# Attention and MoE kernel: decoding of a weight tile spread over a pair, phi's transposes one pair later, last transposes between h pieces

## The chip, the core and the metric

One core of a Trainium2 chip. The kernel is one program for its engines: TensorE (PE) for matmuls and transposes, VectorE (DVE), ScalarE (ACT), GpSimd (POOL), and SyncE (SP) as the queue of most DMAs. Each engine takes its own instructions in a fixed order. The metric is the time of one execution on the device in microseconds (us), the median of several runs.

## The reference, cut to what matters

Attention with a causal softmax and a linear-attention memory, then two MLPs, all in float32. `H` = 8 heads and `B` = 4 make 32 (b, head) blocks of 576 rows; `w_in` is 512x2048, `w_out` 2048x512.

```
scores = scale * q @ k.T;  causal mask;  a = softmax(scores)
local = a @ v
phi(x) = where(x > 0, x, exp(x) - 1) + 1
mem_out = (phi(q) @ M_prev) / (phi(q) . z_prev + 1e-6)
x = g * mem_out + (1 - g) * local            # g = sigmoid(beta), 2304 rows of 512
h = x @ w_in;  y = (h * tanh(softplus(h))) @ w_out
out = ((y @ w1) * (y @ w2)) @ w3 @ w_out2
```

## The kernel before

**Stages.** The 32 blocks are 16 pairs (two heads of one b, one on each half of the partitions). A software pipeline runs over `p` = 0 to 16: while the scores of pair p are made, pair p-1 is transposed and multiplied with v. Then follow 24 units of the first MLP (4 quarters of `w_in` and `w_out` by 6 chunks of 384 tokens; `emit_h` makes h and its activation, `emit_x2` the second matmul), beside which w3 and w_out2 are multiplied (`fold`), and at the end the second MLP. A float32 matmul is three in a reduced format, so most operands exist as a high and a low part.

**A pair.** `s_blocks` (L380) and `s_last` (L396) make scores in PSUM, tile `psA`: row blocks 3, 2, then 0 and 1, then the last 64 rows of both heads (128x576, in two halves of 288). For each block DVE scales, masks and takes the row extremum (`maxed`, L372, 128x512, 384, 128, 256, 288), and ACT takes the exp and its row sum (`expd`, L377, L378). `normed` (L357) then scales each block by the gate over its sum: a short sum (L363) and reciprocal (L364) on DVE, four blocks on DVE and four on POOL (L368), and the last block (128x576) on DVE at the very end. One pair later `pt_g` (L421) transposes these blocks on PE into a bank `psF` and ACT copies them out (L430). `pv` (L432) accumulates memory and local part in `psX` and `psF`; ACT copies the high part (L451) and DVE subtracts for the low part (`xt`, L79 called from L452). `prep` (L306) transposes q and k of the next pair into `psX` (copied by ACT, L308) and makes `qd` on POOL (L314).

**Phi.** `prep_phi` (L322) works on the next pair's q: exp on ACT (L330), `phit` on POOL (L331), `phie` on DVE (L332), `qz` on POOL (L334), its row reduction `dn` on DVE (L338), `dn` + 1e-6 on POOL (L339), reciprocal and a product of 128x10 on DVE (L340, L341), and the scaled phi on POOL (L344). `trans_phi` (L349) transposes it on PE into two `psX` tiles, each copied by ACT (L351). All of it belongs to the end of p, for pair p+1.

**Decoding.** The weights come as 64-bit words and are turned into float32 by `decode` (L103): a DMA of 512 KB into `draw`, six DVE operations of 128x512 (L113, L115, L117, L120, L124, L126), one POOL addition (L131), and, for the first MLP, the rounding and subtraction on POOL that give the two parts (`to_split`, L148). The eight tiles of quarter 0 (`lq0`) are decoded at p = 3, 6, 9 and 12 in the code, one each, with one buffer, and the last four at p = 16 with a decoder of their own.

**What sets the order.** The code is written in one order, and a scheduler, from its own estimate of durations, sets the order in which each engine takes its instructions. `tc.issue_after(ins)` keeps what is issued inside it behind `ins` in that order; `in_turn` uses it to put PE's work of the pairs behind PE's last instruction. DMAs stand in SP's queue in that order too. The scheduler places the four tiles of p = 3 to 12 beside pairs 1 to 4. A `psA`, `psX` or `psF` tile is one of two buffers and is free again when the last reader of the old content is through.

## Time and profile before

| | |
|---|---|
| runs | 1026.53, 1024.01, 1025.31 us; median 1025.31 |
| profiled execution | 1024.95 us, span 1023.2, mean granted clock 0.988 |
| busy, of the span | PE 977.8 us (96%), DVE 612.0 (60%), ACT 500.7 (49%), POOL 339.0 (33%) |
| attention, first matmul of h | at 246.93 us |
| first matmul of `emit_x2` | at 277.37 us |
| chain that ended last | PE 71%, DVE 12%, ACT 11% |

Times in the trace are microseconds from the span's start. A row of the timeline has the start, the duration, engine, line, operation, output <- inputs, shape and count (a merged row holds several like it), and in brackets the idle time of that engine just before, with what ended it. A row of a window has the busy time of each engine in it, and the granted clock of PE as a share of the full one. The share of busy time over the whole span is an average over stages with different limits; the stages are read apart below.

### The profile page before, as it was taken

The page shows a single profiled execution, that of the slowest core. Times are in us where ns is not written, and L with a number is a line of the kernel's source. Part 1 is how long each engine was busy: PE and PEld are TensorE (multiplying, and loading weights), DVE is VectorE, ACT ScalarE, POOL GpSimd, SP SyncE. Part 2 cuts the span into 40 slices and gives each one's busy share as a digit, 9 for nine tenths or more (in the row PEclk, how much of TensorE's full clock was granted, in tenths as well). Part 3 has the DMA queues.
Part 4 walks back from the last instruction along what each step waited for, and adds up shares of the span by engine and source line. Part 5 has one row for each costly group of instructions (what it writes and reads, how often), then busy time and mean ns, then how long its engine had stood idle before and what let it go on. Part 6 is the DMA issues. An engine that isn't in the chain of part 4 may idle for free.

```text
span 1023.2 us, 15086 instructions
## 1 busy us (share of the span) xinstructions
PE 977.8 (96%) x5584; PEld 829.1 (81%) x5584; DVE 612.0 (60%) x1364; ACT 500.7 (49%) x1016; POOL 339.0 (33%) x345
## 2 busy tenths in 40 slices
PE   5888999999899999999999999999979999999998
PEld 2555555566799999999999999988758888888897
DVE  4887667667685759885987567667973121121111
ACT  5577888885655555556565544442313221221212
POOL 6675555433555254544454112112540000000000
PEclk9899999999999999999999999999999999999999
DMA  7343333311232124223331662222410000100101
GB/s 157 96 110 71 71 87 74 77 27 42 103 124 80 65 83 145 98 89 106 121 103 63 247 232 80 75 78 101 156 41 1 21 21 1 42 1 1 42 1 62
DMA packets 93626, 81.73 MB, mean 80 GB/s; under 512 B 68720, under 2 KB 72816, under 8 KB 93552
## 3 DMA queue, kind: packets, MB, share of 16 engines
q1 hardware_dynamic: 92224, 80.44, 25.3%
q8 instruction: 44, 0.72, 0.3%
q10 hardware_dynamic: 1328, 0.33, 0.2%
q14 instruction: 30, 0.25, 0.1%
HBM read 65.54 MB, written 15.20 MB: 79 GB/s over the span
## 4 chain that ended last, share of the span: by engine, by line
PE 71%; DVE 12%; ACT 11%; DMA 2%; POOL 2%; issue 2%; SPq 0%; POOLq 0%; ACTq 0%; DVEq 0%
PE psA L63 37%; PE psX L63 16%; PE psF L63 14%; ACT s L378 5%; ACT pt L430 3%; DVE s L368 2%; PE psF L66 2%; DMA draw<-in_moe_w_dram 1%; DVE da L120 1%; PE psX L66 1%; DVE xt L79 1%; POOL da L131 1%; DVE draw L126 1%; DVE da L117 1%; DVE s L373 1%
## 5 line engine op out<-in xcount | busy, mean ns | idle before, releaser
L63 PE MATMUL psA<-xt,wqt 128*128 128x384 f32 x1152 | 207.5, 335 | 0.2
L131 POOL TENSOR_TENSOR da<-da,draw 128x512 f32<-128x512 f32 x72 | 102.2, 1426 | 312.8 <-DVE draw L126 261.9
L63 PEld LDWEIGHTS psA<-xt,wqt 128*128 128x128 f32 x1152 | 200.0, 188 | 2.4 <-DVE y L487 0.8
L63 PE MATMUL psX<-gh,wqt 128*128 128x384 f32 x480 | 122.4, 335 | 1.1 <-DVE x L604 1.1
L749 DVE TENSOR_TENSOR bs<-bs,psA 128x512 f32<-128x512 f32 (+1 forms) x40 | 25.3, 633 | 160.0 <-ACT bs L748 160.0
L63 PE MATMUL psA<-x2h,w12t 128*128 128x512 f32 (+1 forms) x384 | 107.1, 356 | 6.9 <-DVE bs L749 4.6
L748 ACT COPY bs<-psA 128x512 f32<-128x512 f32 (+1 forms) x40 | 21.8, 545 | 162.1 <-PE psA L63 152.2
L378 ACT ACTIVATE s<-s,acc 128x512 f32<-128x512 f32 (+2 forms) x144 | 85.5, 603 | 12.8 <-DVE acc L373 12.7
L63 PE MATMUL psA<-x2s,w12t 128*128 128x512 f32 x384 | 89.6, 389 | 0.0
L63 PEld LDWEIGHTS psX<-gh,wqt 128*128 128x128 f32 x480 | 86.9, 188 | 2.3 <-DVE x L604 1.4
L477 ACT ACTIVATE y<-psA 128x384 f32<-128x384 f32 x96 | 42.0, 490 | 91.1 <-PE psA L63 91.0
L63 PEld LDWEIGHTS psA<-x2h,w12t 128*128 128x128 f32 x384 | 68.3, 189 | 20.7 <-DVE bs L749 5.0
L63 PEld LDWEIGHTS psA<-x2s,w12t 128*128 128x128 f32 x384 | 72.1, 188 | 14.9
L373 DVE CUSTOM_DVE_ANT_0 s<-psA,mask 128x512 f32<-128x512 f32 (+2 forms) x144 | 63.4, 483 | 34.4 <-PE psA L63 34.3
L63 PE MATMUL psX<-gl,wqt 128*128 128x384 f32 x240 | 80.3, 335 | 0.0
L66 PEld LDWEIGHTS psF<-ident,s 128*128 128x128 f32 x400 | 46.3, 147 | 40.8 <-ACT pt L430 24.8
L63 PE MATMUL psF<-gh,wqt 128*128 128x384 f32 x288 | 73.1, 334 | 0.0
L66 PE MATMUL psF<-ident,s 128*128 128x128 f32 x400 | 63.2, 292 | 9.9 <-ACT pt L430 7.5
L487 DVE TENSOR_TENSOR y<-y,psA 128x384 f32<-128x384 f32 x96 | 48.7, 549 | 34.9 <-ACT y L485 34.9
L63 PE MATMUL psA<-room,w12t 128*128 128x512 f32 (+1 forms) x192 | 68.0, 354 | 0.0
L368 POOL TENSOR_SCALAR s<-s,sum,ogp 128x128 f32<-128x128 f32 (+1 forms) x64 | 53.1, 840 | 37.2 <-DVE sum L364 37.2
L430 ACT COPY pt<-psF 128x512 f32<-128x512 f32 (+1 forms) x112 | 56.8, 546 | 16.0 <-PE psF L66 16.0
(114 smaller groups left out, 1878.3 us busy)
## 6 DMA issues: line engine op xcount, KB each, us to landing
draw<-in_moe_w_dram SPq DMA_DIRECT2D x32, 512.0 KB, 3.8
draw<-in_moe_w_out_dram SPq DMA_DIRECT2D x24, 512.0 KB, 3.5
draw<-in_moe_w_in_dram SPq DMA_DIRECT2D x16, 512.0 KB, 4.0
out_dram<-ob SPq DMA_DIRECT2D x18, 256.0 KB, 2.0
raw<-in_q_dram SPq DMA_DIRECT2D x32, 128.0 KB, 2.8
raw<-in_v_dram SPq DMA_DIRECT2D x32, 128.0 KB, 2.6
o_dram<-draw SPq DMA_DIRECT2D x8, 512.0 KB, 2.8
w_dram<-draw SPq DMA_DIRECT2D x8, 512.0 KB, 2.8
```

Of the source, the lines that this page charges most:

```text
L63: tail[0] = nc.tensor.matmul(o, lhsT=l, rhs=r, start=start, stop=stop).ins
L66: tail[0] = nc.tensor.transpose(o, src, ident).ins
L79: return (eng or nc.vector).tensor_tensor(out=dst, in0=src, in1=f(hi), op=ALU.subtract)
L131: nc.gpsimd.tensor_tensor(out=a, in0=a, in1=lw.bitcast(F32), op=ALU.add)
L368: (nc.gpsimd if x in ON_POOL else nc.vector).tensor_scalar(out=s, in0=s, scalar1=d["sum"][:, x:x + 1], scalar2=og[:, x:x + 1], op0=ALU.mul ...
L373: nc.vector.tensor_tensor_reduce(out=s, in0=o, in1=m, op0=ALU.add, op1=ALU.min, scale=-scale, scalar=init, accum_out=a,)
L378: nc.scalar.activation(out=s, in_=s, func=AF.Exp, scale=-1.0, bias=a, accum_out=r)
L430: nc.scalar.copy(out=t[:, 0:n], in_=o[:, 0:n])
L477: nc.scalar.activation(out=y[m // 2][:, m % 2], in_=hp[m], func=AF.Tanh, scale=0.5)
L487: nc.vector.tensor_tensor(out=y[i][:, j], in0=y[i][:, j], in1=hp[2 * i + j], op=ALU.mult)
L748: nc.scalar.copy(out=bs, in_=pb)
L749: nc.vector.tensor_tensor(out=bs, in0=bs, in1=pa, op=ALU.mult)
```

## The change

Four things are changed, all in the attention pipeline and its tail.

1. *Decoding.* `decode` is split into `fetch` (the DMA) and `decode_ops` (a list of the six DVE operations and the POOL addition). All eight tiles of quarter 0 are fetched one at a time at p = 3 to 10 and decoded at p = 4 to 11: `drip` issues one operation behind the reduces of each score block (behind `taken`, the last reduce issued), and the remaining ones at the end of the pair. The decoder has two raw buffers; no tile is decoded at p = 16.
2. *Phi.* `prep_phi(p + 1)` is placed behind the last reduce of p, `dn`'s reduction behind the last split of `pv` (`split_x`). `trans_phi(p)` runs one pair later, at the end of pair p itself, with one `psX` and one `psF` bank.
3. *The long norm* (128x576) is placed behind `split_x`.
4. *The tail.* `emit_h` is a generator `h_steps`; at p = 16 its four pieces (one of 12 matmuls for each `m`) alternate with the transposes of pair 15, and ACT's first Sin stands behind the last copy of these (`copied`).

```diff
-        for lw, hw, a, ai, _ in ts:
-            V.tensor_scalar(out=ai, in0=hw, scalar1=0x7FFFFFFF, scalar2=None, op0=ALU.bitwise_and)
...
+    def fetch(src):
+        r = dec["pool"].tile([128, dec["w"], 2], I32, tag="draw", name="draw", bufs=dec["raw"])
+        dm(out=r.rearrange("p n t -> p (n t)"), in_=src)
+        return r
...
-    decoder(at, 1, 1)
+    decoder(at, 2, 1)
...
-    def trans(src, evac):
-        for c0, c1 in ((0, 256), (256, S)):
-            pt = psX()
+    def trans(src, evac, tags="XX"):
+        for tag, (c0, c1) in zip(tags, ((0, 256), (256, S))):
+            pt = bank(tag)
...
-        nc.vector.tensor_reduce(out=dn, in_=qz, axis=mybir.AxisListType.X, op=ALU.add)
+        with ExitStack() as k_:
+            if split_x[0] is not None:
+                k_.enter_context(tc.issue_after(split_x[0]))
+            nc.vector.tensor_reduce(out=dn, in_=qz, axis=mybir.AxisListType.X, op=ALU.add)
...
-        trans(st[p]["e"], lambda cs, o: nc.scalar.copy(out=t[:, cs], in_=o))
+        trans(st[p]["e"], lambda cs, o: nc.scalar.copy(out=t[:, cs], in_=o), "XF")
...
-            if m == 1:
-                steps(beside, 1)
+            yield
...
+        with ExitStack() as k_:
+            if u == (0, 0):
+                k_.enter_context(tc.issue_after(copied[0]))
+            first = nc.scalar.activation(out=d, in_=y[1][:, 1, 0:1], func=AF.Sin, scale=0.0)
...
+    def drip(n):
+
+        if not parts and ahead:
+            r, done = ahead.pop(0)
+            ops, a, flat = decode_ops(r)
+
+            def last():
+                ops[6]()
+                done(a, flat)
+
+            parts.extend(ops[0:6] + [last])
+        with tc.issue_after(taken[0]):
+            for op in parts[:n]:
+                op()
+        del parts[:n]
...
+        decodes = 4 <= p < 12
+        if 3 <= p < 11:
+            fetch_next()
         if now:
             in_turn(s_blocks, p, (3,))
+            if decodes:
+                drip(1)
         else:
-            split = split_y((0, 0), emit_h((0, 0)))
+            in_turn(next, h0)
...
-        if not now:
-            run(lq0, 2)
-            run(lq0, 2)
+            if not now:
+                in_turn(next, h0)
...
+        if p == 1:
+            in_turn(trans_phi, 0)
...
         if p == 0:
-            in_turn(trans_phi, 0)
-        if p in (3, 6, 9, 12):
-            run(lq0, 1)
+            with tc.issue_after(taken[0]):
+                prep_phi(0)
...
+        if now:
+            with ExitStack() as k_:
+                if old:
+                    k_.enter_context(tc.issue_after(split_x[0]))
+                normed(p, [(4, None)])
+            if decodes:
+                drip(7)
         if new:
-            prep_phi(p + 1)
-            in_turn(trans_phi, p + 1)
-        if now:
-            normed(p, [(4, None)])
-    lk.close()
+            with tc.issue_after(taken[0]):
+                prep_phi(p + 1)
+        if now and p > 0:
+            in_turn(trans_phi, p)
```

How the instructions stand then, at the places that matter below. In these rows `s_998` and the like are single tiles of scores; lines are those of each kernel.

DVE at the end of a steady pair before, from the last two reduces to the next pair's first:

```order
L363 TENSOR_SCALAR sum<-sum 128x8
L364 RECIPROCAL sum<-sum 128x8
L368 TENSOR_SCALAR s_998<-s_998,sum,ogp 128x256
L368 TENSOR_SCALAR s_946<-s_946,sum,ogp 128x384
L368 TENSOR_SCALAR s_995<-s_995,sum,ogp 128x128
L368 TENSOR_SCALAR s_949<-s_949,sum,ogp 128x384
L363 TENSOR_SCALAR sum<-sum 128x1
L364 RECIPROCAL sum<-sum 128x1
L79 TENSOR_TENSOR xt_81<-psX,xt_81 128x512
L368 TENSOR_SCALAR s_113<-s_113,sum,ogp 128x576
L79 TENSOR_TENSOR xt_81<-psF,xt_81 128x64
L332 SCALAR_TENSOR_TENSOR phie<-phie,phit 128x640
```

The same place after, in a pair without decoding:

```order
L342 SCALAR_TENSOR_TENSOR phie<-phie,phit 128x640
L376 TENSOR_SCALAR sum<-sum 128x8
L377 RECIPROCAL sum<-sum 128x8
L381 TENSOR_SCALAR s_597<-s_597,sum,ogp 128x256
L381 TENSOR_SCALAR s_545<-s_545,sum,ogp 128x384
L381 TENSOR_SCALAR s_594<-s_594,sum,ogp 128x128
L381 TENSOR_SCALAR s_548<-s_548,sum,ogp 128x384
L79 TENSOR_TENSOR xt_81<-psX,xt_81 128x512
L79 TENSOR_TENSOR xt_81<-psF,xt_81 128x64
L376 TENSOR_SCALAR sum<-sum 128x1
L351 TENSOR_REDUCE dn<-qz 128x10
L377 RECIPROCAL sum<-sum 128x1
```

And after in a pair that decodes a tile (L117, L120 and L121 are decode operations):

```order
L117 SCALAR_TENSOR_TENSOR da<-draw,da 128x512
L342 SCALAR_TENSOR_TENSOR phie<-phie,phit 128x640
L376 TENSOR_SCALAR sum<-sum 128x8
L120 TENSOR_SCALAR draw<-da 128x512
L377 RECIPROCAL sum<-sum 128x8
L121 SCALAR_TENSOR_TENSOR draw<-draw 128x512
L381 TENSOR_SCALAR s_1184<-s_1184,sum,ogp 128x256
L381 TENSOR_SCALAR s_1131<-s_1131,sum,ogp 128x384
L381 TENSOR_SCALAR s_1181<-s_1181,sum,ogp 128x128
L381 TENSOR_SCALAR s_1134<-s_1134,sum,ogp 128x384
L79 TENSOR_TENSOR xt_81<-psX,xt_81 128x512
L79 TENSOR_TENSOR xt_81<-psF,xt_81 128x64
```

Phi's operation (L332, now L342) moved from behind the norms to ahead of the sum, and `dn`'s reduction from the next pair's start to behind the split of `xt`; in decoding pairs three decode operations stand between.

POOL over one pair before:

```order
L334 TENSOR_TENSOR qz<-phie,zr 128x640
L339 TENSOR_SCALAR dn<-dn 128x10
L344 TENSOR_TENSOR phie<-phie,dn 128x640
L314 TENSOR_TENSOR qd<-qt,own 128x128
L331 TENSOR_SCALAR phit<-raw 128x640
L368 TENSOR_SCALAR s_1372<-s_1372,sum,ogp 128x128
L368 TENSOR_SCALAR s_1303<-s_1303,sum,ogp 128x512
L368 TENSOR_SCALAR s_1381<-s_1381,sum,ogp 128x256
L368 TENSOR_SCALAR s_1306<-s_1306,sum,ogp 128x512
```

POOL over one pair after, without decoding:

```order
L352 TENSOR_SCALAR dn<-dn 128x10
L341 TENSOR_SCALAR phit<-raw 128x640
L357 TENSOR_TENSOR phie<-phie,dn 128x640
L324 TENSOR_TENSOR qd<-qt,own 128x128
L344 TENSOR_TENSOR qz<-phie,zr 128x640
L381 TENSOR_SCALAR s_783<-s_783,sum,ogp 128x128
L381 TENSOR_SCALAR s_714<-s_714,sum,ogp 128x512
L381 TENSOR_SCALAR s_792<-s_792,sum,ogp 128x256
L381 TENSOR_SCALAR s_717<-s_717,sum,ogp 128x512
```

The same nine operations; `qz` stands directly ahead of the four norms, where it stood ahead of `dn`, behind the norms of the pair before.

ACT at the start of a pair before:

```order
L330 ACTIVATE phie<-raw 128x640
L430 COPY pt<-psF 128x512 x2
L378 ACTIVATE s_1303,sum<-s_1303,acc 128x512
L378 ACTIVATE s_1306,sum<-s_1306,acc 128x512
L430 COPY pt<-psF 128x512 x2
L378 ACTIVATE s_1326,sum<-s_1326,acc 128x384
L308 COPY qt<-psX 128x256
L308 COPY qt<-psX 128x320
L378 ACTIVATE s_1329,sum<-s_1329,acc 128x384
```

ACT at the start of a pair after:

```order
L340 ACTIVATE phie<-raw 128x640
L447 COPY pt<-psF 128x512
L395 ACTIVATE s_2703,sum<-s_2703,acc 128x512
L447 COPY pt<-psF 128x512
L395 ACTIVATE s_2706,sum<-s_2706,acc 128x512
L447 COPY pt<-psF 128x512
L395 ACTIVATE s_2726,sum<-s_2726,acc 128x384
L447 COPY pt<-psF 128x512
L318 COPY qt<-psX 128x256
L395 ACTIVATE s_2729,sum<-s_2729,acc 128x384
L318 COPY qt<-psX 128x320
```

The copies of the old pair's transposed blocks (`pt`) and of `qt` now alternate with the exps; before, two copies stood ahead of the first exp.

PE in the tail before, from the matmuls of h (`psA<-xt`) on:

```order
L63 MATMUL psA<-xt_81,wqt 128x384 x45
L66 MATMUL psF<-ident,s_3074 128x128
L66 MATMUL psF<-ident,s_3036 128x128
L66 MATMUL psF<-ident,s_3013 128x128 x2
L66 MATMUL psF<-ident,s_3068 128x128
L66 MATMUL psF<-ident,s_3074 128x128
L66 MATMUL psF<-ident,s_3036 128x128
L66 MATMUL psF<-ident,s_3013 128x128
L66 MATMUL psF<-ident,s_3036 128x128
```

PE in the tail after:

```order
L63 MATMUL psA<-xt_81,wqt 128x384 x12
L66 MATMUL psF<-ident,s_3112 128x128
L66 MATMUL psF<-ident,s_3074 128x128
L66 MATMUL psF<-ident,s_3051 128x128 x2
L66 MATMUL psF<-ident,s_3106 128x128
L66 MATMUL psF<-ident,s_3112 128x128
L66 MATMUL psF<-ident,s_3074 128x128
L66 MATMUL psF<-ident,s_3051 128x128
L63 MATMUL psA<-xt_81,wqt 128x384 x12
L66 MATMUL psF<-ident,s_3074 128x128
L66 MATMUL psF<-ident,s_3051 128x128
```

The first unit of h, 48 matmuls ahead of nearly all transposes before, stands in four pieces of 12 between them.

## Rows read from the trace of the kernel before

**Rows 1.** Windows, core 0, by stage (start:end, length, busy of each engine, granted clock, DMA).

```profile
26.18:46.36 20.18, 15.43 (x103) 9.60 (x104) 17.71 (x46) 11.74 (x34) 13.66 (x16) 0.84 0.45 114
...
97.20:237.07 139.87, 132.73 (x1023) 82.45 (x1020) 95.18 (x349) 116.04 (x339) 70.71 (x85) 1.00 0.29 65
246.93:277.37 30.44, 27.85 (x188) 22.98 (x186) 20.00 (x36) 14.47 (x26) 15.62 (x14) 0.94 0.26 90
277.37:1023.20 745.83, 733.77 (x3857) 672.72 (x3856) 419.44 (x741) 300.32 (x454) 185.66 (x160) 1.00 0.23 79
```

**Rows 2.** Timeline of DVE, one steady pair (start, duration, what, idle before).

```profile
124.41 0.83 DVE L332 SCALAR_TENSOR_TENSOR phie<-phie,phit 128x640 f32<-128x640 f32 x1 [1.17 <-ACT phie L330]
125.16 0.68 DVE L373 CUSTOM_DVE_ANT_0 s<-psA,mask 128x512 f32<-128x512 f32 x1
...
126.91 0.82 DVE L338 TENSOR_REDUCE dn<-qz 128x10 f32<-128x640 f32 x1 [0.45 <-POOL qz L334]
...
132.59 0.52 DVE L373 CUSTOM_DVE_ANT_0 s<-psA,mask,acc 128x288 f32<-128x288 f32 x1
...
134.17 1.45 DVE L368 TENSOR_SCALAR s<-s,sum,ogp 128x256 f32<-128x256 f32 x4
...
135.88 0.69 DVE L79 TENSOR_TENSOR xt<-psX,xt 128x512 fp32r<-128x512 f32 x1
136.48 0.61 DVE L368 TENSOR_SCALAR s<-s,sum,ogp 128x576 f32<-128x576 f32 x1
```

**Rows 3.** Timeline of POOL, the same pair.

```profile
125.32 1.55 POOL L334 TENSOR_TENSOR qz<-phie,zr 128x640 f32<-128x640 f32 x1 [1.57 <-DVE phie L332]
...
134.31 3.33 POOL L368 TENSOR_SCALAR s<-s,sum,ogp 128x128 f32<-128x128 f32 x4 [2.18 <-DVE sum L364]
```

**Rows 4.** Timeline of ACT, the same pair, its start.

```profile
125.94 0.72 ACT L378 ACTIVATE s<-s,acc 128x512 f32<-128x512 f32 x1
...
127.37 1.05 ACT L430 COPY pt<-psF 128x512 f32<-128x512 f32 x2
128.31 0.62 ACT L378 ACTIVATE s<-s,acc 128x384 f32<-128x384 f32 x1
...
128.92 0.69 ACT L308 COPY qt<-psX 128x256 f32<-128x256 f32 x2
```

**Rows 5.** Timeline of DVE, then of POOL, pair 1.

```profile
31.61 1.51 DVE L341 TENSOR_TENSOR dn<-dn,gates 128x10 f32<-128x10 f32 x1
...
31.45 1.65 POOL L334 TENSOR_TENSOR qz<-phie,zr 128x640 f32<-128x640 f32 x1 [1.71 <-DVE phie L332]
```

**Rows 6.** By line, 20 to 300 us: three decode operations on DVE (ns minimum/median/maximum).

```profile
L120 DVE SCALAR_TENSOR_TENSOR da<-draw,da x12: 675/688/1634, 33.5 to 294.4; 128x512 int32<-128x512 int32 x12
...
L124 DVE TENSOR_SCALAR draw<-da x12: 370/427/1084, 36.9 to 295.3; 128x512 int32<-128x512 int32 x12
...
L126 DVE SCALAR_TENSOR_TENSOR draw<-draw x12: 684/694/1705, 37.7 to 296.3; 128x512 f32<-128x512 uint32 x12
```

**Rows 7.** Timeline of PE in pairs 4 and 6, and the window of pair 4.

```profile
84.80 0.66 PE L66 MATMUL psF<-ident,s 128*128 128x128 f32 x4 [2.02 <-ACT pt L430]
...
88.23 1.98 PE L63 MATMUL psA<-kt,qd 128*128 128x288 f32 x4
...
130.91 1.14 PE L63 MATMUL psA<-kt,qd 128*128 128x288 f32 x4
...
86.52:89.93 3.41, 3.41 (x14) 2.98 (x13) 1.04 (x8) 3.41 (x14) 2.86 (x4) 0.50 0.53 121
```

**Rows 8.** Timeline of DVE, first reduce of pair 15.

```profile
236.28 0.69 DVE L373 CUSTOM_DVE_ANT_0 s<-psA,mask 128x512 f32<-128x512 f32 x1 [1.69 <-PE psA L63]
```

**Rows 9.** Timeline of PE, the tail.

```profile
248.80 8.07 PE L63 MATMUL psA<-xt,wqt 128*128 128x384 f32 x45
...
258.31 1.15 PE L66 MATMUL psF<-ident,s 128*128 128x128 f32 x8 [0.57 <-ACT pt L430]
...
262.44 1.14 PE L66 MATMUL psF<-ident,s 128*128 128x128 f32 x8 [1.98 <-ACT pt L430]
```

More of the change, by code (lines that the diff above doesn't have):

```diff
@@ L134, in run, with decode @@
+    def decode(srcs):
+        ts = [decode_ops(fetch(src)) for src in srcs]
+        for i in range(6):
+            for ops, _, _ in ts:
+                ops[i]()
+        for ops, a, flat in ts:
+            ops[6]()
+            yield a, flat
     def run(jobs, n):
@@ L370, in normed @@
             )
+    taken = [None]
+    split_x = [None]
+    copied = [None]
     def maxed(s, o, m, init, a):
-        nc.vector.tensor_tensor_reduce(
+        taken[0] = nc.vector.tensor_tensor_reduce(
             out=s, in0=o, in1=m, op0=ALU.add, op1=ALU.min, scale=-scale, scalar=init, accum_out=a,
-        )
+        ).ins
     def expd(s, a, r):
@@ L429, in pt_g @@
             d.setdefault("t", {})[ib, e, jb] = t[:, 128 * x:128 * x + 128] if e is None else (t, 128 * x)
-        nc.scalar.copy(out=t[:, 0:n], in_=o[:, 0:n])
+        copied[0] = nc.scalar.copy(out=t[:, 0:n], in_=o[:, 0:n]).ins
     def pv(p):
@@ L487, in emit_h @@
                 nc.vector.tensor_tensor(out=y[i][:, j], in0=y[i][:, j], in1=hp[2 * i + j], op=ALU.mult)
+        yield y
+    def emit_h(u, beside=iter(())):
+        for m, y in enumerate(h_steps(u)):
+            if m == 1:
+                steps(beside, 1)
         return y
@@ L512, in fused_kernel, with fetch_next @@
     lq0 = load_quarter(0)
+    ahead = []
+    parts = []
+    def fetch_next():
+        for src, done in islice(lq0, 1):
+            ahead.append((fetch(src), done))
+    def drip(n):
[3 more added lines that the diff above has]
+            def last():
+                ops[6]()
+                done(a, flat)
[4 more added lines that the diff above has]
+        del parts[:n]
     pre = predecode()
@@ L522, in fused_kernel @@
             wps[0] = wk.enter_context(tc.tile_pool(name="wp", bufs=1, side="right"))
-            lk = ExitStack()
-            decoder(lk, 2, 2, side="right")
+            h0 = h_steps((0, 0))
         if p + 2 < NPAIR:
@@ L545, in fused_kernel @@
             in_turn(pt_g, p - 1, 2)
+            if not now:
+                in_turn(next, h0)
         if new:
@@ L551, in fused_kernel @@
             in_turn(s_blocks, p, (0, 1))
+            if decodes:
+                drip(1)
         if new:
@@ L556, in fused_kernel @@
             in_turn(pt_g, p - 1, 6)
+            if not now:
+                in_turn(next, h0)
+        if p == 1:
+            in_turn(trans_phi, 0)
         if now:
             in_turn(s_last, p)
+            if decodes:
+                drip(1)
             normed(p, [(i, e) for e in range(2) for i in range(4)])
         if p == 0:
-            in_turn(trans_phi, 0)
-        if p in (3, 6, 9, 12):
-            run(lq0, 1)
+            with tc.issue_after(taken[0]):
+                prep_phi(0)
         if old:
```

54 lines of the change are left out of this document (26 added, 28 removed).

## Prediction

> **What bounds the kernel now.** I read the windows by stage first [rows 1]. From 277.37 us to the end TensorE (PE) is busy 733.77 of 745.83 us: that part can't get shorter by this change, and whatever the first 277 us gain or lose moves the end one for one. Of these the ten pairs from 97.20 to 237.07 take 13.95 us each (139.87 / 10) with PE busy 132.73 of 139.87 us at a granted clock of 1.00: PE-bound too. The first pairs are not: pair 1's window takes 20.18 us with PE at 15.43, and DVE, which there also decodes a tile, at 17.71. In the tail (246.93 to 277.37) PE is busy 27.85 of 30.44 us at a mean clock of 0.94. So there are two places with slack, the early pairs and the tail, and one place, the steady pairs, with none to lend on PE but much on DVE (95.18 of 139.87) and POOL (70.71). The change takes decoding out of the first two and puts it into the third, where idle engine time looks ample. The question is not busy time but the order in a pair's end.
>
> Next I read one steady pair on each engine [rows 2 to 4]. From the start of its first 128x512 reduce (125.16) a pair runs to the last two reduces (the second at 132.59), then sum, reciprocal, four norms (134.17, x4, 1.45), the split of the PV result (135.88) and the long norm (136.48). Phi's preparation (`L332`, `L334`, `L338`) lies at the *start* of the pair: POOL's `qz` (125.32, 1.55) runs while DVE reads scores from PSUM, and DVE takes the result up at 126.91, behind an idle of 0.45 us. POOL's four norms (134.31, 3.33) start 0.14 us after DVE's.
>
> **SBUF operations of DVE and POOL hold each other up** [rows 5, 6]. DVE's product of 128x10 numbers at 31.61 takes 1.51 us: it ends at 33.12, when POOL's `qz` (31.45 + 1.65 = 33.10) ends. It is too small to need that of itself. The decode step `L120` of before takes 688 ns in the median, and 1634 ns at most. Reduces out of PSUM show nothing of the kind: the one at 125.16 has `qz` beside it from 125.32 on, takes 0.68 us, and the next operations follow it without a gap until 126.46.
>
> **The pair in the new order.** Operations of DVE start about 0.08 us before the one ahead ends in its row (124.41 + 0.83 against 125.16), so I take each row less 0.08. The walk goes from one first 512-reduce to the next. Lines here are those of the changed kernel: phi's `L342`, `L344`, `L351` were `L332`, `L334`, `L338`, and the decode steps `L117`, `L120`, `L121` were `L120`, `L124`, `L126`.
> 1. ACT. The copies of the old pair's transposed blocks now stand between the exps. Before, two of them were done by 125.94, ahead of the first exp. Exps and copies by [rows 4], from the first reduce to the last copy of `qt`: reduce 0.70, exp 0.72, copy 0.50, exp 0.72, copy 0.50, exp 0.61, copy 0.47, copy `qt` 0.30, exp 0.61, copy `qt` 0.28, together 5.4 us. Behind it PE has the last transposes of k (0.42), of the old pair (0.70) and the last scores (1.18; 1.14 in the row at 130.91 [rows 7]): the last reduces start 7.7 us after the first. Before it was 6.9 (the first of the two at 132.09).
> 2. The two last reduces 1.02, then `L342` 0.75. This releases POOL's `qz`, which now stands *ahead* of POOL's norms, not behind them. So DVE's sum (0.17) passes, and then the norms wait for `qz`, 1.54. Norms 1.36, the PV splits 0.81, a second sum 0.16, the reduce of `qz` 0.75, a reciprocal 0.15, the long norm 0.53. Then dn goes to POOL and back (0.27), a reciprocal 0.24, and its product (0.17) waits behind POOL's next `phit`, 0.42. (These last small ones are estimates, from 0.15 to 0.25 us a piece in the steady pair.) Together 1.02 + 7.3 = 8.3 us.
> Sum: 7.7 + 8.3 = 16.0, with hand-overs 16.1 us for a pair without decoding. The same walk over the order of before gives 13.9 against the 13.95 measured.
> 3. A pair with a decoded tile. Behind the last reduces DVE now has `L117` 0.61 ahead of `L342`, and `L120` 0.36 and `L121` 0.62 between sum and norms (medians of rows 6 less 0.08). The long norm and dn's three operations move behind the next 512-reduces: 0.61 + 0.75 + 0.17 + 1.54 + 0.36 + 0.62 + 1.36 + 0.81 + 0.16 + 0.75 + 0.15 = 7.3. With 1.02 and 7.7 that is 16.0 again. `L110`, `L111`, `L114` lie in DVE's waits for PE, but for about 0.4 us of `L111` and `L114`, which stand right ahead of the last reduces: 16.5. POOL's three decode operations (1.28, 0.61, 1.27) fall beside DVE's PSUM reads.
>
> **The sum**, against the profiled run's 1024.95 us (span 1023.2; it stands 0.4 below the median).
> - Start: pair 0 loses phi's preparation and its transposes, pair 1 its decoded tile. Its first reduce, at 26.18, comes about 2 us sooner, and a plain pair's 16.1 us follow in place of 20.18: pair 2's first reduce at 40.4 in place of 46.36, -6.
> - Pairs 2 to 14: the first reduces of pairs 2 (46.36) and 15 (236.28 [rows 8]) are 189.9 us apart before. After: 5 pairs x 16.1 + 8 x 16.5 = 212.5, +22.6. In this the early pairs' decoding (three more tiles, in pairs 2 to 4) is already gone.
> - Tail: h twice at 8.07 us, 25 transposes of 0.145 (3.6) and the rest of PV (4.2) are 23.9 us of PE work in 30.4. The waits for ACT's copies, 0.57 and 1.98 [rows 9], go when h pieces lie between them; four decoded tiles leave DVE and POOL; and the mean clock of 0.94, which costs 1.8 us of 30.44, goes up with the waits gone. Of the 6.5 us I take 5: -5. The new h pieces hold `psA`; ACT's Tanh waits behind the last copies, as the added wait of Sin on `copied` says, and ACT has 14.47 busy of 30.44, so nothing is charged.
> - Clock falls in pairs that now hold idle time. One such fall before: PE waits 2.02 at 84.80, and the clock is 0.50 from 86.52 to 89.93; the last scores then take 1.98 in place of 1.14 [rows 7], with the transposes beside them about 1.2 us on the path. The new pair leaves PE some 2.7 us idle of 16.3. I take a fall in one pair of three: 4 x 1.2, +4.
> - At nothing: the tiles' DMAs. They stand in SP's queue behind a pair's q, k and v loads, two raw buffers let each wait for a tile that is decoded a pair earlier, and no load of the next pairs is due within its wait; if SP did stop there, the cost would be one late q load, once per tile, of up to its 3 us. `trans_phi`'s second half takes an F bank, and so loses a short wait on the split at each pair's end; it is no term, since DVE is late there now.
> -6 + 22.6 - 5 + 4 = +15.6: **1040 us**. Pairs 2 to 14 would break even at (189.9 + 11 - 4) / 13 = 15.1 us.
>
> **Rivals.**
> - *The clock falls in every pair.* For: the long early pairs show falls (mean clock 0.84 in pair 1's window, 0.50 for 3.4 us in pair 4), the ten at 13.95 none. Against: those pairs had their idle time in one or two stretches behind a run of decode steps. 13 x 1.2 = 15.6 in place of 4: 1052. The Trainium skill, "TensorE: Matmul & The Clock Gate", section "A second HAM failure mode: psum-queue depth-cycling", says that short idles between matmul groups can make the clock swing between its two levels; by that rule this is the likeliest case, while a steady pair here keeps 1.00 with its short idles.
> - *The other side: the norms aren't held* (faster). If neither `qz` nor POOL's order delays DVE's norms, say because `qz` finds the pair's SBUF access taken and POOL's norms are not due before the next PE blocks, the walk gives 14.4 and 14.8 us: 5 x 14.4 + 8 x 14.8 = 190.4, +0.5, and with -11 and no clock falls 1014.5. It decides as soon as a pair is under 15.1. For: DVE idles a third of a steady pair and POOL half. Against: the 1.51 at 31.61.
> - *DVE's norms go first, POOL's come late.* Then `qz` waits 1.4 for the norms, POOL's own norms 3 us more; the old pair's first two transposes want them. About 15.1 and 15.3: 5 x 15.1 + 8 x 15.3 = 197.9, +8 - 11 + 1: 1023, no change. The Trainium skill, "SBUF — State Buffer", section "Who interferes with whom", has it that whichever of the two engines issues first keeps the shared ports for its whole instruction. By that rule the 0.2 us between `qz` and the first norm decide between 1040 and this 1023; in the order listed the reciprocal leaves `qz` the gap.
> - *The tail doesn't gain*: if what bounds it is the chain of ACT copies and Tanh, 1045.
>
> **How the numbers follow.** Chances: forecast 0.50 (1030 to 1047), a fall in every pair 0.15, norms not held 0.16, norms first 0.12, no tail gain 0.07. The range leaves out the 0.16 and the top half of the clock's case: 1019 to 1052. A measurement of this kernel can tell about 0.3%, 3.1 us, from no change: faster is under 1022.2, slower over 1028.4. Faster: 0.16 and a third of "norms first", 0.20. Same: 0.07. Slower: 0.73.
>
> **What would show it.** Right: in the new trace the first reduces of pairs 6 to 11 lie 16 to 17 us apart; DVE's four norms (1.45 before) show 2.5 to 3 us or start when POOL's `qz` ends; POOL's norms start behind `qz`; the tail from the first h matmul to the first of x2 takes 24 to 27 us; the part behind it is unchanged at 746. Wrong: a period under 15.1 us, `qz` beside reduces or behind the norms, or the tail at 30.

## The result, and the profile after

The changed kernel takes 1032.05 us (median of 4 runs, 1029.42 to 1032.55) against 1024.96 us (4 runs, 1024.01 to 1026.53): a ratio of 1.0062, 95% interval 1.0044 to 1.008, so it is slower, by 6 or 7 us (0.6%). The forecast was 1040. The profiled execution is the shortest of the four, 1029.42 us (span 1027.6), so the two traces are 4.5 us apart; where the other 2.6 us can come from is told at the end.

The windows by stage of the changed kernel answer to [rows 1]: pairs 2 and 3, pairs 4 to 11 (with decoding), pairs 12 to 14, pair 15 up to the first matmul of h, the tail from there to the first matmul of x2 (the second matmul of the first MLP), and the rest. The single row behind them is the kernel before, from pair 15's first reduce to the first matmul of h. The columns are those of [rows 1].

```profile
39.98:70.40 30.42, 27.14 (x210) 16.75 (x207) 21.53 (x71) 23.46 (x68) 14.70 (x19) 1.00 0.33 73
70.40:196.17 125.77, 108.72 (x814) 65.56 (x814) 109.14 (x327) 94.75 (x272) 84.90 (x93) 1.00 0.39 95
196.17:241.68 45.51, 40.24 (x310) 24.96 (x310) 33.42 (x111) 34.72 (x101) 25.21 (x31) 1.00 0.14 31
241.68:253.96 12.28, 10.44 (x79) 6.72 (x77) 6.76 (x28) 8.93 (x27) 3.80 (x5) 0.86 0.00 0
253.96:281.92 27.96, 25.46 (x167) 23.15 (x164) 10.65 (x25) 14.84 (x26) 2.44 (x3) 0.94 0.16 57
281.92:1027.60 745.68, 733.75 (x3857) 672.74 (x3856) 412.60 (x730) 300.06 (x454) 182.13 (x159) 1.00 0.23 78
```

```profile
236.28:246.93 10.65, 10.01 (x61) 5.63 (x60) 6.98 (x29) 8.84 (x26) 1.97 (x3) 1.00 0.11 37
```

The window limits are the starts of first 128x512 reduces, so they give the account: pair 2 begins at 39.98 in place of 46.36, -6.4 us. Pairs 2 to 14 take 241.68 - 39.98 = 201.7 us in place of 189.9, +11.8; a plain pair takes about 15.2 us (30.42 / 2, 45.51 / 3), a decoding one 15.7 (125.77 / 8), where a steady pair took 13.95. From pair 15's first reduce to x2 it is 281.92 - 241.68 = 40.24 in place of 41.09 (277.37 - 236.28), -0.85: up to the first matmul of h +1.63 (12.28 for 10.65), behind it -2.48 (27.96 for 30.44). The rest is 745.68 in place of 745.83. Together +4.4, which is the distance of the two traces. So a gain at the start and next to none in the tail are paid for with more in the pairs, and PE is at full clock all through pairs 2 to 14. Pair 15 and the tail have stretches at half clock (means of 0.86 and 0.94).

The end of a plain pair on DVE (pair 13), then POOL at the same place; this answers to [rows 2, 3]:

```profile
219.23 0.46 DVE L390 CUSTOM_DVE_ANT_0 s<-psA,mask 128x288 f32<-128x288 f32 x1 [1.62 <-PE psA L63]
...
219.74 0.52 DVE L390 CUSTOM_DVE_ANT_0 s<-psA,mask,acc 128x288 f32<-128x288 f32 x1
...
220.18 0.82 DVE L342 SCALAR_TENSOR_TENSOR phie<-phie,phit 128x640 f32<-128x640 f32 x1
220.91 0.17 DVE L376 TENSOR_SCALAR sum<-sum 128x8 f32<-128x8 f32 x1
...
221.36 2.46 DVE L381 TENSOR_SCALAR s<-s,sum,ogp 128x256 f32<-128x256 f32 x4
223.74 0.68 DVE L79 TENSOR_TENSOR xt<-psX,xt 128x512 fp32r<-128x512 f32 x1
...
224.53 0.80 DVE L351 TENSOR_REDUCE dn<-qz 128x10 f32<-128x640 f32 x1
...
226.37 0.54 DVE L354 TENSOR_TENSOR dn<-dn,gates 128x10 f32<-128x10 f32 x1
226.83 0.68 DVE L390 CUSTOM_DVE_ANT_0 s<-psA,mask 128x512 f32<-128x512 f32 x1
...
221.08 1.55 POOL L344 TENSOR_TENSOR qz<-phie,zr 128x640 f32<-128x640 f32 x1 [3.46 <-DVE sum L376]
222.62 2.96 POOL L381 TENSOR_SCALAR s<-s,sum,ogp 128x128 f32<-128x128 f32 x4
```

From the last reduces on DVE has no idle time to the next pair's first: no row behind 219.23 has a bracket. Its four norms take 2.46 us in place of 1.45, and POOL's `qz` runs from 221.08 to 222.63, across their start. POOL's norms start behind `qz`. The product of 128x10 takes 0.54 us beside `phit`.

Not all of the added time lies there. Pair 13 takes 15.22 us, 1.28 more than a steady pair before. From its first reduce (211.61) to the last two it takes 7.62 us, where the pair of [rows 2] takes 6.93 (125.16 to 132.09): +0.69, in the part in which ACT's copies now stand between the exps. From the last two reduces to the next pair's first it takes 7.60 us in place of 7.01 (132.09 to 139.10): +0.59, the part with `phie`, `qz` and the norms; there the waits for ACT that DVE had before (0.61 us ahead of the sum, 1.13 ahead of `phie`) are gone, and the longer chain has taken their place. The rows are the last reduces and the next first reduce of the pair of [rows 2], and the first reduce of pair 13:

```profile
132.09 0.46 DVE L373 CUSTOM_DVE_ANT_0 s<-psA,mask 128x288 f32<-128x288 f32 x1 [1.34 <-PE psA L63]
...
139.10 0.68 DVE L373 CUSTOM_DVE_ANT_0 s<-psA,mask 128x512 f32<-128x512 f32 x1
```

```profile
211.61 0.68 DVE L390 CUSTOM_DVE_ANT_0 s<-psA,mask 128x512 f32<-128x512 f32 x1
```

In a decoding pair another operation meets `qz` (pair 8; DVE, then POOL):

```profile
143.67 1.92 DVE L121 SCALAR_TENSOR_TENSOR draw<-draw 128x512 f32<-128x512 uint32 x1
145.51 1.74 DVE L381 TENSOR_SCALAR s<-s,sum,ogp 128x256 f32<-128x256 f32 x4
...
147.95 0.80 DVE L351 TENSOR_REDUCE dn<-qz 128x10 f32<-128x640 f32 x1
...
143.30 1.73 POOL L344 TENSOR_TENSOR qz<-phie,zr 128x640 f32<-128x640 f32 x1 [4.07 <-DVE sum L376]
```

`L121` is the operation that took 694 ns in the median before [rows 6]. Here it takes 1.92 us and ends 0.56 us after `qz`.

### The profile page after: what moved, and what is told of

The parts are those of the page before. It is cut to its first block, busy times and chain, and to the rows that moved or that the text cites. A ratio compares the mean times of both kernels' runs of the same rounds, so it can differ in the third digit from the quotient of the medians.

```text
span 1027.6 us, 15098 instructions
## 1 busy us (share of the span) xinstructions
PE 974.8 (95%) x5584; PEld 827.7 (81%) x5584; DVE 617.1 (60%) x1364; ACT 501.4 (49%) x1016; POOL 336.8 (33%) x345
## 4 chain that ended last, share of the span: by engine, by line
PE 69%; DVE 15%; ACT 6%; DMA 3%; POOL 3%; issue 2%; SPq 1%; POOLq 0%; DVEq 0%; ACTq 0%
PE psA L63 37%; PE psX L63 15%; PE psF L63 14%; DVE s L390 2%; ACT s L395 2%; DVE draw L121 2%; DVE s L381 1%; PE psF L66 1%; ACT pt L447 1%; DVE da L117 1%; DMA draw<-in_moe_w_dram 1%; PE psX L66 1%; DVE phie L342 1%; DVE y L506 1%; DVE draw L120 1%
## 5 line engine op out<-in xcount | busy, mean ns | idle before, releaser
L66 PE MATMUL psF<-ident,s 128*128 128x128 f32 x400 | 66.4, 292 | 23.8 <-ACT pt L447 14.9
L63 PEld LDWEIGHTS psA<-x2s,w12t 128*128 128x128 f32 x384 | 72.1, 188 | 14.9
L447 ACT COPY pt<-psF 128x512 f32<-128x512 f32 (+1 forms) x112 | 58.9, 540 | 17.7 <-PE psF L66 17.6
L63 PE MATMUL psX<-wft,room 128*128 128x512 f32 x216 | 61.6, 391 | 0.3 <-DVE wft L79 0.3
```

Source lines behind the costliest of these rows:

```text
L63: tail[0] = nc.tensor.matmul(o, lhsT=l, rhs=r, start=start, stop=stop).ins
L66: tail[0] = nc.tensor.transpose(o, src, ident).ins
L447: copied[0] = nc.scalar.copy(out=t[:, 0:n], in_=o[:, 0:n]).ins
```

## The experiments

Lines in the experiments' traces are some numbers off those of the changed kernel; the tiles' names tell what is what. The diffs are cut to the lines that matter, with the experiments' switches written out. Periods below are distances of first 128x512 reduces: "plain" is the mean of pairs 12 to 14 (15.2 in the changed kernel), "decoding" pairs 4 to 11 (15.7), "from pair 15" the distance from its first reduce to the end of the span (786.9 us before, 785.9 in the changed kernel).

### The three parts alone

The kernel before with one part each.

drip_only:

```diff
-        if p in (3, 6, 9, 12):
-            run(lq0, 1)
...
-            run(lq0, 2)
-            run(lq0, 2)
...
+        if 3 <= p < 11:
+            fetch_next()
...
+            if 4 <= p < 12:
+                drip(1)
```

phi_only:

```diff
         if now:
+            with ExitStack() as k_:
+                if old:
+                    k_.enter_context(tc.issue_after(split_x[0]))
                 normed(p, [(4, None)])
         if new:
-            prep_phi(p + 1)
-            in_turn(trans_phi, p + 1)
+            with tc.issue_after(taken[0]):
+                prep_phi(p + 1)
+        if now and p > 0:
+            in_turn(trans_phi, p)
```

tail_only:

```diff
-            split = split_y((0, 0), emit_h((0, 0)))
+            in_turn(next, h0)
...
             in_turn(pt_g, p - 1, 0)
+            if not now:
+                in_turn(next, h0)
```

> Before, with the spread decoding alone (one tile in each of pairs 4 to 11, none in pairs 1 to 4, none in the tail); phi, the long norm and the tail's order as before. Theory (what costs in the changed kernel is phi's qz ahead of the norms, and decoding only the 0.55 us by which its decoding pairs, 15.75 us, stand over its plain ones, 15.2): pairs 12 to 14 at 13.95, decoding pairs at about 14.5, 8 x 0.55 = +4.4; the early pairs lose four tiles, 71.0 us for pairs 1 to 4 before against 4 x 14 to 15, -11 or more; about 1017 us. Rival (decoding beside the pairs is the cost): decoding pairs at 15.5 or more, +12 to +14 and -11: 1025 to 1028 us.

> Before, with phi's preparation, dn's reduction, phi's transposes and the long norm placed as in the changed kernel; decoding and tail as before. Theory (qz ahead of the norms): DVE's four norms 2.4 us in place of 1.45, pairs without decoding at 15.2 in place of 13.95, for ten pairs and more +12 to +16, less some 2 us at the start: 1035 to 1040 us. Rival (decoding is the cost): pairs at 13.95 to 14.2, 1023 to 1027 us.

> Before, with the tail's order alone changed (h pieces between the transposes, Sin behind the last copy); four tiles still decoded in the tail. Theory (the interleaving ends h later, so ACT's chain from Tanh to Sin lies bare and the next h waits for psA): PE waits about 2 us for y ahead of the second unit of h and the clock falls behind that; from the first reduce of pair 15 to the first x2 matmul 41 us or more, as before (41.1): 1024 to 1028 us. Rival (the interleaving gains the waits for ACT's copies, 2.5 us, and the clock's 1.8): 36 to 38 us, 1020 to 1022 us.

| run | median us (n) | ratio, interval | plain | decoding | from pair 15 |
|---|---|---|---|---|---|
| drip_only | 1039.09 (4) | 1.0136, 1.0109 to 1.0162 | 13.9 | 15.2 to 18.5 | 788.0 |
| phi_only | 1048.85 (4) | 1.0227, 1.0206 to 1.0248 | 15.1 | none | 792.3 |
| tail_only | 1025.58 (10) | 1.0010, 0.9999 to 1.0020 | 13.8 | none | 786.6 |

*drip_only* goes past both expectations. The spread decoding is far dearer here (15.2 to 18.5 us a pair, 17.3 on average) than in the changed kernel (15.7). One reason is at the first score block (pair 8; DVE, then POOL):

```profile
139.29 1.75 DVE L111 TENSOR_SCALAR da<-draw 128x512 int32<-128x512 int32 x1 [0.66 <-POOL wqt L80]
140.96 0.54 DVE L403 CUSTOM_DVE_ANT_0 s<-psA,mask 128x384 f32<-128x384 f32 x1
...
139.21 1.54 POOL L352 TENSOR_TENSOR qz<-phie,zr 128x640 f32<-128x640 f32 x1
```

The first decode operation waits until POOL has freed the one buffer (`wqt`), meets `qz` there, and takes 1.75 us; the 128x384 reduces stand behind it on DVE, and so ACT's exps and PE. In this kernel the clock does fall in the pairs: the window of pair 7 (119.46 to 137.34) has a mean granted clock of 0.90, and so has that of pairs 5 to 11 (85.21 to 208.17).

*phi_only* has the plain pairs of the changed kernel, 15.2 us each for nine pairs running (5 to 13), with the norms at 2.45 us and without a decode operation beside them. So phi's new place (with the order of ACT's copies that comes with it), not decoding, makes a pair 15.2 us: the theory. Of the rest of its loss, 5.4 us lie behind pair 15's first reduce (792.3 for 786.9 us, with a granted clock of 0.92 up to x2 and 0.99 behind it), and some 8 us are one pair of 28.3 us near the start, where DVE stands 4.49 us for a decoded tile's transfer with the pair's reduces behind it:

```profile
27.62 0.43 DVE L111 TENSOR_SCALAR da<-draw 128x512 int32<-128x512 int32 x1 [4.49 <-DMA draw<-in_moe_w_in_dram]
```

*tail_only* is the kernel before, within what can be measured: theory. From pair 15's first reduce to the first matmul of x2 it takes 36.75 us, which would be the rival's mark, but here x2 starts with 24 of the second unit's 48 matmuls still to come, so that mark doesn't tell the two apart; the whole time does. PE waits for y ahead of the second unit of h, 4.37 us where the theory had about 2:

```profile
266.31 6.02 PE L64 MATMUL psA<-xt,wqt 128*128 128x384 f32 x24 [4.37 <-DVE y L519]
```

These 24 take 6.02 us, the next 24 take 4.32: the fall of the clock that the theory had.

### qz ahead of the last scores

```diff
+        if new and p > 0:
+            with tc.issue_after(taken[0]):
+                phi_head(p + 1)          # exp, phit, phie, qz of prep_phi
         if now:
             in_turn(s_last, p)
...
             with tc.issue_after(taken[0]):
-                prep_phi(p + 1)
+                phi_tail(p + 1)          # dn, its product, the scaled phi
```

> The changed kernel, with the next pair's exp, phit, phie and qz ahead of the last scores of the pair instead of behind their reduces. Theory (qz beside DVE's norms, and phie in the chain, cost the pair): DVE's phie and POOL's qz fall into DVE's wait for the last scores (1.62 us), the four norms take 1.45 us again, plain pairs at 14.0 to 14.2 in place of 15.2, decoding pairs at 14.5 to 14.9 in place of 15.75, 13 pairs save 13 us: about 1018 us. Rival (ACT's new order of copies and exps, by which the last scores come 7.6 us after the first in place of 6.9, holds the pair): 14.9 or more for a plain pair, 1027 us or more.

1015.96 us (4 runs), ratio 0.9909, 0.989 to 0.9928: 0.9% faster than the kernel before, 16 us under the changed kernel. In the traces pairs 2 to 14 take 188.6 us in place of 201.7; 13.1 us of the gain are there. Plain pairs take 13.70, 14.23 and 13.95 us (12 to 14), decoding ones 14.75. Pair 13 on DVE, then POOL:

```profile
206.00 0.82 DVE L347 SCALAR_TENSOR_TENSOR phie<-phie,phit 128x640 f32<-128x640 f32 x1
207.70 0.46 DVE L403 CUSTOM_DVE_ANT_0 s<-psA,mask 128x288 f32<-128x288 f32 x1 [0.88 <-PE psA L64]
...
209.08 1.45 DVE L394 TENSOR_SCALAR s<-s,sum,ogp 128x256 f32<-128x256 f32 x4
...
206.89 1.54 POOL L352 TENSOR_TENSOR qz<-phie,zr 128x640 f32<-128x640 f32 x1 [0.81 <-DVE phie L347]
```

`phie` now lies where DVE waited 1.62 us for the last scores (0.88 us of the wait are left), `qz` ends at 208.43, and the norms are back at 1.45 us. From the last two reduces (207.70) to the next pair's first (214.30) it is 6.60 us in place of 7.60: the whole gain of the pair. Behind the norms DVE now waits 0.96 us for ACT's copy of the PV result, so they no longer bound it there. The rival falls with 14.23 us, under its 14.9. Its mechanism hasn't gone, though: from the first reduce (200.07) to the last two it is still 7.63 us, 0.7 more than before the change. No run puts ACT's old order back by itself, so how much of these 0.7 us is ACT's order is not shown.

The run moves `phie` and `qz` together; what each is worth alone it doesn't tell.

### qz left out, and qz behind the norms

no_qz:

```diff
-        nc.gpsimd.tensor_tensor(
-            out=qz, in0=e, in1=z[:, None, :, :].to_broadcast([128, NB, 2, D]), op=ALU.mult
-        )
...
-            nc.vector.tensor_reduce(out=dn, in_=qz, axis=mybir.AxisListType.X, op=ALU.add)
+            nc.vector.tensor_reduce(out=dn, in_=e, axis=mybir.AxisListType.X, op=ALU.add)
```

qz_late, where `pooled` is POOL's last norm of the pair:

```diff
+        with tc.issue_after(pooled[0]):
             nc.gpsimd.tensor_tensor(
                 out=qz, in0=e, in1=z[:, None, :, :].to_broadcast([128, NB, 2, D]), op=ALU.mult
             )
```

> The changed kernel without POOL's product qz (dn is reduced over phie instead, so the memory part's norm is left out). phie still stands behind the last reduces on DVE. Theory (POOL's qz holds DVE's norms, phie adds its own 0.75 us): the four norms take 1.45 us again and start 0.3 us sooner or at once, a plain pair takes 14.1 to 14.4 us in place of 15.2, a decoding pair 14.7 to 15.2 in place of 15.75; about 1018 us. Rival (phie's place or ACT's order alone): norms 1.45 but pairs at 15.0 or more.

> The changed kernel with qz behind POOL's four norms instead of ahead of them; phie stays behind the last reduces. Theory (moving qz alone only trades one wait for another: the norms are free, but dn's reduction, which stands ahead of the next pair's 128x512 reduces, then waits for POOL's 3.3 us of norms and 1.55 of qz): DVE's four norms 1.4 to 1.5 us in place of 2.46, an idle of about 1 us or more on DVE ahead of dn's reduction, a plain pair at 15.2 to 15.6 us in place of 15.2. Rival (qz's place ahead of the norms is the whole cost): plain pairs at 14.2 us.

*no_qz*: one run, 1023.29 us; the plain pairs 2 and 3 take 14.49 and 14.50 us (15.21 in the changed kernel), 12 to 14 take 15.21, 14.50 and 13.96 (15.44, 15.22 and 14.85), decoding ones 15.48. The norms aren't back at 1.45. With `qz` gone POOL's `phit`, 0.72 us, stands in its place. Pair 13 on DVE (the four norms, then the first of them by itself) and on POOL:

```profile
215.65 2.29 DVE L394 TENSOR_SCALAR s<-s,sum,ogp 128x256 f32<-128x256 f32 x4
...
215.65 0.67 DVE L394 TENSOR_SCALAR s<-s,sum,ogp 128x256 f32<-128x256 f32 x1
...
215.45 0.72 POOL L346 TENSOR_SCALAR phit<-raw 128x640 f32<-128x640 f32 x1 [3.54 <-DVE sum L389]
216.16 2.79 POOL L394 TENSOR_SCALAR s<-s,sum,ogp 128x128 f32<-128x128 f32 x4
```

The first norm of pair 13 in the changed kernel:

```profile
221.36 1.42 DVE L381 TENSOR_SCALAR s<-s,sum,ogp 128x256 f32<-128x256 f32 x1
```

The first norm is 0.75 us shorter without `qz`. But the three behind it, which lie beside POOL's norms in both kernels, take 1.69 us (216.25 to 217.94) where they take 1.12 in the changed kernel (222.70 to 223.82); there it is POOL's first norm that is slower (0.70 us for 0.47). What decides which of the two engines is held there is not shown. So the four gain 0.17 us only, and most of the 0.72 us by which pair 13 is shorter comes from elsewhere: the product of 128x10 no longer has `phit` beside it (the next pair's first reduce starts 0.09 us after it in place of 0.46), and the reciprocal ahead of it, which waited for POOL's `dn` + 1e-6, starts 0.49 us after the long norm in place of 0.68. This run thus doesn't tell what `qz` costs the norms. The expectation's numbers are not met, and neither are the rival's norms of 1.45.

*qz_late*: one run, 1038.53 us; pairs 12 to 14 take 15.42, 14.96 and 16.25 us, decoding ones about 16.5. The last of the plain ones and the decoding ones have stretches at half clock in them (means of 0.89, and 0.91 from 104.71 to 203.24), pairs 12 and 13 have none. Pair 12 on DVE:

```profile
212.98 1.45 DVE L397 TENSOR_SCALAR s<-s,sum,ogp 128x256 f32<-128x256 f32 x4
...
217.93 0.82 DVE L367 TENSOR_REDUCE dn<-qz 128x10 f32<-128x640 f32 x1 [1.42 <-POOL qz L355]
```

The norms are free, and DVE waits 1.42 us for `qz` instead, ahead of the next pair's reduces. The rival (14.2 us) falls: `qz`'s place before the norms is not the whole cost. Once `phie` stands behind the last reduces, `qz` and `dn` have to pass between these and the next pair's first, on one side of the norms or the other.

### Where the decode operations stand

drip_later (on the base of drip_only) and qe_later (on the base of qe_midtail, below):

```diff
             in_turn(s_blocks, p, (3,))
-            if decodes:
-                drip(1)
...
             in_turn(s_blocks, p, (2,))
-            if decodes:
-                drip(1)
...
             in_turn(s_blocks, p, (0, 1))
             if decodes:
-                drip(1)
+                drip(3)
```

qe_da2 (on the base of qe_midtail):

```diff
-    decoder(at, 2, 1)
+    decoder(at, 2, 2)
```

> The run with the spread decoding alone, with the first three decode operations of a tile together behind the reduces of row blocks 0 and 1 (before: one behind each score block). Theory (the first operation waits for POOL to free the tile's buffer and then for qz, 1.75 us in place of 0.35, and the 128x384 reduces, ACT's exps and PE stand behind it): decoding pairs at 15.5 to 16.2 us in place of 16.5 to 18.5, about 1025 us. Rival (the sum of decode work on DVE, wherever it stands): 17.3 or more, 1037 us.

> The run with phie and qz ahead of the last scores and the tail's h pieces sooner, with the first three decode operations of a tile behind the reduces of row blocks 0 and 1. Theory (those operations lay in DVE's wait for PE and were free there; now they stand beside phie, ahead of the last reduces and the norms): decoding pairs longer, 15.2 to 15.8 us in place of 14.75. Rival (the first of them, 1.47 us beside POOL's product, holds the pair): 14.3 us or less.

> The run with phie and qz ahead of the last scores and the tail's h pieces sooner, with two buffers for a decoded tile. Theory (a decoding pair's 14.75 us come from the three decode operations between the last reduces and the norms, 2.0 us less what DVE idled there): still 14.6 to 14.8 us. Rival (the first decode operation waits for POOL to free the one buffer, and the 128x128 reduces wait behind it): 14.2 to 14.4 us, 1011 us.

*drip_later*: one run, 1024.61 us, decoding pairs 15.0 to 16.0, on average 15.6 in place of 17.3: with the first operation out of the reduces' way the old order loses 1.7 us less a pair, as the theory had it, and the granted clock is 1.00 in all these pairs, where drip_only had 0.90, so a part of the 1.7 us is the clock's. *qe_later*: one run, 1018.98 us, decoding pairs 15.05, 0.3 us worse than with the first operation in DVE's wait for PE, though less than expected. *qe_da2*: one run, 1020.57 us and 15.23 us, which neither side expected. With a second buffer the scheduler puts the first decode operation ahead of the product that POOL's last phi operation needs:

```profile
147.91 0.42 DVE L111 TENSOR_SCALAR da<-draw 128x512 int32<-128x512 int32 x1
148.25 1.24 DVE L367 TENSOR_TENSOR dn<-dn,gates 128x10 f32<-128x10 f32 x1
149.41 0.55 DVE L403 CUSTOM_DVE_ANT_0 s<-psA,mask 128x384 f32<-128x384 f32 x1
```

The product of 128x10 then lies beside a POOL operation of 1.41 us and takes 1.24, with the reduces behind it: the first of 128x384 comes 2.66 us after the pair's first reduce (146.75), 1.25 in qe_midtail. So the run changes two things, the buffer and the order, and settles neither side.

### The tail

The changed kernel's tail, PE, then ACT, then DVE:

```profile
263.50 2.36 PE L63 MATMUL psA<-xt,wqt 128*128 128x384 f32 x12
...
271.92 10.15 PE L63 MATMUL psA<-xt,wqt 128*128 128x384 f32 x48 [2.20 <-DVE y L506]
...
265.90 0.87 ACT L493 ACTIVATE y<-psA 128x384 f32<-128x384 f32 x2 [1.85 <-PE psA L63]
266.79 1.28 ACT L499 ACT_TABLE_LOAD   x1
...
269.84 1.74 ACT L504 ACTIVATE y<-y,halfpi 128x768 f32<-128x768 f32 x2
...
270.85 1.95 DVE L506 TENSOR_TENSOR y<-y,psA 128x384 f32<-128x384 f32 x4 [15.68 <-ACT y L504]
```

The waits of [rows 9] are gone. But the last piece of h ends at 265.86, and only then can ACT go from Tanh through the table load to Sin; both `psA` tiles are held until DVE's product at 270.85. PE has PV to do meanwhile, then waits 2.20 us, and the second unit takes 10.15 us with the clock at half for part of it, where one of 48 takes 8.5.

The trace of qz_early has the same order here and the same wait of 2.20 us, but no half clock. From pair 15's first reduce to the first matmul of h, and from there to x2, it has:

```profile
228.25:239.34 11.09, 10.07 (x83) 6.05 (x82) 6.77 (x28) 9.26 (x28) 3.88 (x5) 1.00 0.00 0
239.34:265.73 26.39, 23.90 (x166) 21.59 (x165) 10.65 (x25) 14.85 (x26) 0.82 (x2) 1.00 0.17 61
```

That is 37.5 us together, where the changed kernel takes 40.24 and the kernel before 41.09. So in the changed kernel's trace 2.8 us of this stretch (1.19 and 1.57) go to the clock. Two runs on the base of qz_early change only the tail's order:

qe_midtail:

```diff
             in_turn(pt_g, p - 1, 0)
             if not now:
                 in_turn(next, h0)
+                in_turn(next, h0)
...
             in_turn(pt_g, p - 1, 6)
-            if not now:
-                in_turn(next, h0)
```

qe_oldtail:

```diff
-            in_turn(next, h0)
+            split = split_y((0, 0), emit_h((0, 0)))
```

> The run with phie and qz ahead of the last scores, with the tail's h pieces sooner: one, 8 transposes, two, 8 transposes, one, 9 transposes and PV (there: one piece after each 8 or 9). Theory (the second unit of h waits for psA, which the first holds until ACT has gone from Tanh to Sin): the chain starts 1.3 us sooner, PE's wait for y falls from 2.2 to about 1 us: 1014.5 to 1015 us. Rival (ACT's copies of transposes are what the tail waits for): the wait stays at 2, 1016 us or more.

> The run with phie and qz ahead of the last scores, with the tail's order as before the change (the whole first unit of h ahead of the transposes, no constraint on Sin), still without decoding in the tail. Theory (the interleaving trades the waits for ACT's copies, 2.5 us, against the wait for psA, 2.2 us): 37 to 39 us from the first reduce of pair 15 to the first x2 matmul, as with it (37.5): 1015.5 to 1017.5 us. Rival (the interleaving is a gain of its own): 40 us or more, 1018 us or more.

qe_midtail: 1015.42 us (4 runs), ratio 0.9908, 0.989 to 0.9927; the wait for y is 1.59 us in place of 2.20, less of a gain than expected:

```profile
256.82 8.59 PE L64 MATMUL psA<-xt,wqt 128*128 128x384 f32 x48 [1.59 <-DVE y L519]
```

qe_oldtail: 1016.69 us (4 runs), ratio 0.992, 0.9903 to 0.9936; 38.9 us from pair 15's first reduce to x2, against 37.5 with the interleaving. So the interleaving is worth 1.4 us in the traces, and the medians of the three (1015.4, 1016.0, 1016.7) can't be told apart.

## Why the prediction was right and wrong

- **What failed** is a size. The forecast was +15.6 us; +7 came in the medians and +4.4 in the traces. The step that failed is the walk over one pair in the new order, 16.1 and 16.5 us, from which the term of pairs 2 to 14 is made: +22.6 was +11.8. Two smaller terms failed too, the tail (-5, measured -0.85) and the clock falls in the pairs (+4, none seen), and these two nearly cancel.
- **The direction and its mechanism** were right. `qz` ahead of the norms and beside them, the norms at 2.46 us, POOL's norms late, DVE's chain without a gap, the last reduces 7.6 us after the first: as forecast. By the Trainium skill, "SBUF — State Buffer", section "Who interferes with whom", where an instruction of DVE uses the ports that it shares with POOL, the engine that issues first keeps them for its whole instruction. The trace agrees: here `qz`, issued 0.28 us before the norms, delays them by 1.0 us. By the same section of the Trainium skill a reduction (`tensor_reduce`) on DVE never takes part in this. The trace agrees here too: DVE's reduction of 128x640 at 224.53 us takes 0.80 us beside POOL's norms, and 0.82 in [rows 2], with POOL idle.
- **Pairs 2 to 14** are the term mis-sized most, by 10.8 us: 16.1 and 16.5 us a pair were 15.2 and 15.7. In a plain pair step 1 of the walk held (7.7 us to the last reduces; 7.62, from pair 13's first reduce at 211.61 to 219.23). Step 2 was 8.3 us and took 7.6 (226.83 - 219.23), and the 0.1 for hand-overs isn't there either. The largest piece is the wait for `qz`, taken at its full 1.54: `qz` was under way for 0.28 us when the norms started, so sum, wait and norms were 2.83 (220.91 to 223.74) in place of 3.07. The product behind `phit` was 0.46 in place of 0.59, the way of `dn` to POOL and back, 0.27, lay mostly beside the long norm, and most of the other rows are up to a tenth shorter. Over 5 plain and 8 decoding pairs this is the miss. In a decoding pair (pair 8) `qz` holds the decode operation `L121` (1.92 us) more than the norms (1.74); from the sum to the split it is 4.03 us where the walk had 4.05, and the miss is in the rows around it. The check that the walk gave 13.9 us for the kernel before said less than it seemed: that pair is held by PE (132.73 of 139.87 us busy, [rows 1]), so DVE's chain was not what it tested.
- **The start** (-6) was -6.4, in part by luck. Pair 1's first reduce came 4.35 us sooner (21.83 for 26.18) where 2 was taken, and pair 1 then took 18.15 us where 16.1 was, at a mean granted clock of 0.87.
- **Decoding** was priced at 0.4 us a pair and took 0.5. That this is phi's doing is not shown: beside the old phi decoding costs up to 4.5 us a pair in drip_only, but with the first three operations later (drip_later) a pair takes 15.6 us there too, no more than in the changed kernel.
- **The tail** (-5) was -0.85. Two things were wrong. First, "nothing is charged" for ACT: ACT is half idle there, but its chain from Tanh to Sin is serial, and interleaving makes h's last piece end later, so the chain lies bare and holds `psA`. A wait of 2.20 us came for the 0.57 and 1.98 that went. Second, the mean clock was to go up with the waits gone; it is 0.94 again, and pair 15 ahead of it, which no term had, has a fall of its own (0.86). By the trace of qz_early, which has the same order at full clock, these falls are 2.8 of the 4.15 us that are missing. That trace has the same wait of 2.20 us, so the wait alone doesn't decide on the fall.
- **Clock falls** (+4) didn't come in pairs 2 to 14 of this trace: 1.00 in all of them, though PE waits some 1.6 us in one piece in each of the plain ones. The rival of a fall in every pair is out; what it describes does happen in drip_only (0.90). The one fall in pair 15 costs the 1.2 us that were taken for one (12.28 us, 11.09 in qz_early).
- **The rivals and the signs.** qz_early comes near the time of "the norms aren't held" (1014.5), but there the norms are free because `phie` and `qz` were moved. "The tail doesn't gain" nearly held as a condition (-0.85); the pairs hid it in the sum. Break-even was put at 15.1 us a pair with 4 us less for the clock. With the tail's -0.85 it is (189.9 + 6.4 + 0.85) / 13 = 15.2; the pairs average 201.7 / 13 = 15.5. Of the signs, POOL's norms behind `qz` and the unchanged 746 us came; the first reduces of pairs 6 to 11 lie 15.7 to 15.9 us apart in place of 16 to 17, and the tail from h to x2 takes 27.96 us in place of 24 to 27.
- The parts by their measured sizes (-6.4 + 11.8 - 0.85 - 0.1) give the profiled 1029.4. The median is 2.6 us above it, with a granted clock of 0.990 to 0.992 in the other runs and 0.993 in the profiled one.

## What to carry to other kernels

An operation moved to where an engine's busy share is low may still land in the one chain that has no slack: look for the wait that it could fill (here 1.6 us ahead of the last scores) and put the producer in front of it, so that its product is through before the next user of the shared resource. Price a change by the difference to a measured stretch that has the same bound; a walk that reproduces a stretch held by another engine is not calibrated, and its small roundings are multiplied by the number of periods. An experiment that takes an operation out lets the next one move up into its place: look at what stands there before its time is read as the price of the one that went. When two things are interleaved so that one ends later, follow what is queued behind its end and which buffers it holds.
